# One core: softmax attention beside a spectral filter; how the first weights are fetched, when a score tile lends its third bank, and the order at the end

## The chip, the cores and the metric

The kernel runs on one core of a Trainium2 chip. The metric is the time of one execution on the device in microseconds (us); the median of four runs of the kernel before is 454.83 us (454.6 to 455.17). TensorE (PE) multiplies matrices into PSUM, which has eight banks of 512 float32 columns; ScalarE (ACT) computes functions, here the exponentials; VectorE (DVE) and GpSimd (POOL) do elementwise work; SyncE (SP) and ScalarE each have a queue for DMAs. The engines run side by side and wait for one another by semaphores.

## What is computed

```python
def _A_ref(x, wqkv, wo):                      # x: 1 x 2048 x 448, 16 heads of 28
    qkv = (x @ wqkv).reshape(B, S, 3, H, Dh)...
    p = softmax(einsum("bhqd,bhkd->bhqk", q, k) * Dh ** -0.5)
    return (p @ v, heads joined) @ wo
def _B_ref(x, w_r, w_i):                      # x: 1 x 2048 x 448
    return irfft2(rfft2(x) * (w_r + 1j * w_i))
out = concatenate([a, b], axis=-1)            # bfloat16
```

## The kernel before

`build_kernel` is its own planner. While it builds the program it keeps an estimated clock for each engine (`P.free`) and writes one instruction stream per engine, waits included; the order on each engine is fixed by then. The costs in the code (`mm_cost`, `cost=`) only steer that order.

**Attention.** The heads are four groups of four. A *unit* is the score of one head for 128 keys and 512 queries, one bank; there are 1024 units. `emit_tile` (its matmuls are L989) issues a tile of two or three units into the banks of its parity: even tiles use banks 0 to 2, odd tiles 3 to 5. One ScalarE instruction (L1002) then exponentiates the whole tile into `ET`, 1024 or 1536 columns, so a tile's banks are refilled while ScalarE works on the other parity's. Some units are not given to ScalarE: `choose` picks them and `start_d`/`finish_d` compute the exponential for pairs of them on DVE and POOL into `DE` (L1028, L1056, L1059, L1063, L1067, L1072, L1077). `emit_pv` (L1113) multiplies four units with V into bank 6; after 16 such groups the sums are normalized (`finish`).

**Jobs.** Everything else that TensorE does is a list of jobs with due times: transposes of x (L380), projections of q, k and v (L434, L452, L469, L486), the transforms of the spectral part (L655, L720, L774, L801, L837) and output projections (`o_job`, L1217). A job needs a bank for its sum: bank 7, or one that a score tile lends. `lend(t)` decides whether tile t gives up its third bank, and is then a two-bank tile; before tile `NT0` = 30 it always does. The lent bank is `lent[0]`. A job that is `SLIP` = 9 slots behind its due time counts as a reason to lend.

**Activity.** The planner adds up what TensorE streamed in the last 3.41 us. Below `TGT` x 4096 it starts jobs ahead of their due times; below `DUM` x 4096, with room left, it issues a filler, a matmul on zeros (`dummy`, L506).

**Head.** SP loads the first quarter of x (L344) and then the q and k columns of `wqkv`, rows 0 to 383, in one DMA (L349); ScalarE's queue loads the identity `cid` (L339) and rows 384 to 447 (L351). Then come the other quarters of x, the v columns, B's x and the constants. TensorE issues fillers, transposes the first quarter of x (L518), issues four fillers, and projects in three steps (`first_mm`, L434): keys 0 to 127 of head group 0, its queries 0 to 511, its other keys. POOL spreads k columns of `wst` into the padded `wk` (`spread`, recorded at L335): first those of group 0, then, after two of the four fills of `Vaug`, those of groups 1 to 3; then it fills `wo` and issues its four loads. Copies go through the helper `copy`, so they carry lines L333 (ACT) and L335 (DVE, POOL).

**Tail.** After the last score tile the main loop goes on until all PV groups and jobs are out. `ahead_o` may issue the first three of the four matmuls of an output tile (L1124) while it waits. `final_finish` handles the last 512 queries: first it finishes a job that is under way, then come the copies of the sums (`oaug`), the sums of the softmax by matmul (L1158), the reciprocals (L1163), their spread (`rzrep`, L1170), the normalized values (`onrm`, L1172), the last output matmuls (L1124), four evacuations and four DMAs.

Of the kernel before, what the change touches and what calls it, by code (L numbers as in the profile page):

```python
# [8 lines left out]
ALU = mybir.AluOpType  # L9
# [187 lines left out]
def build_kernel(nc, A_x, A_wqkv, A_wo, B_x, B_w_r, B_w_i, out):  # L197
    NG = 4
    UN = 1024
# [12 lines left out]
    DT0 = 30  # L212
    EARLY = 1
    TAILU = 8
    TGT = 1.05
    DUM = 0.95
    DROOM = 1.0
    PROOM = 6.0

# [14 lines left out]
    ROOMX = 0.0  # L234
    ZGAP = 9.0
    ALT = 0
    ODUE = 2
    POOLMID = -9.0

# [9 lines left out]

    ZRUN = 5  # L250

    SLIP = 9
    scale = float(DH) ** -0.5
    y16 = scale * 1.4426950408889634 * 65536.0
    bf16np = mybir.dt.np(BF16)
# [13 lines left out]
    ctx = ExitStack()  # L269
    with ctx:  # L270
        sem_names = ["pe", "act", "dve", "pool"]
        sem_names += ["d_x%d" % i for i in range(4)] + ["d_w", "d_wv", "d_wo", "d_c0", "d_c1", "d_t1", "d_t2", "d_xb"]
        sem_names += ["d_f%d" % i for i in range(4)] + ["d_wb%d" % i for i in range(2)] + ["d_o%d" % i for i in range(4)]
        P = Prog(nc, {n: ctx.enter_context(nc.semaphore("s_" + n)) for n in sem_names})

# [66 lines left out]
        def load_x(n):  # L342

            P.dma("sp", lambda e: e.dma_start(xa[:, 4 * n:4 * n + 4, :], A_x[0][512 * n:512 * n + 512, :].rearrange("(p c) d -> p c d", p=128)),  # L344
                  "d_x%d" % n, reads=[("xa", 0)] * (n == 1), writes=[("xa", n)], kb=448)

        load_x(0)
        load_c(0, 1, "cid", "act")
        P.dma("sp", lambda e: e.dma_start(wst[:, 0:3, :], A_wqkv[0:384, 0:896].rearrange("(c p) k -> p c k", p=128)),  # L349
              "d_w", writes=[("w", 0)], kb=672)  # L350
        P.dma("act", lambda e: e.dma_start(wst[64:128, 3, :], A_wqkv[384:448, 0:896]), "d_w", writes=[("w", 1)], kb=112)  # L351
        load_x(1)
        P.dma("sp", lambda e: e.dma_start(wv[:, 0:3, :], A_wqkv[0:384, 896:1344].rearrange("(c p) k -> p c k", p=128)),
              "d_wv", writes=[("wv", 0)], kb=336)
        P.dma("sp", lambda e: e.dma_start(wv[64:128, 3, :], A_wqkv[384:448, 896:1344]), "d_wv", writes=[("wv", 1)], kb=56)
        load_x(2)
        load_x(3)
        load_c(1, 3, "cid2")

        P.op("dve", lambda e: e.memset(zero[:], 0.0), writes=["zero"], cost=0.3)  # L360
# [2 lines left out]
        def spread(eng, g0, g1, part):  # L363

            off = 448 + 112 * g0
            nh = 4 * (g1 - g0)
            if part == 0:
                d_ = wk[:, 0:3, g0:g1, :].rearrange("p c g (j k) -> p c (g j) k", j=4)[:, :, :, 0:DH]
                s_ = wst[:, 0:3, off:off + DH * nh].rearrange("p c (j k) -> p c j k", j=nh)
            else:  # L370
                d_ = wk[64:128, 3, g0:g1, :].rearrange("p g (j k) -> p (g j) k", j=4)[:, :, 0:DH]
                s_ = wst[64:128, 3, off:off + DH * nh].rearrange("p (j k) -> p j k", j=nh)
            copy(eng, d_, s_, [("w", part), "wk", "wk0"], [("wk0" if g0 == 0 else "wk", part)], 0.12 * nh / 4 * (3 - 2 * part) + 0.1)

        def xt_mms(n, hf):
            mms = []
# [65 lines left out]
        def proj_qk(g, n, is_q, due, eng="dve"):  # L442
            mms = []
            if is_q:
                wkeys = [("w", 0), ("w", 1)]
                for c in range(4):
                    mms.append(lambda e, M, c=c: q_mm(e, M, g, c, 512 * n, 512 * (n + 1)))
            else:
                wkeys = [("wk0" if g == 0 else "wk", c) for c in range(2)]
                for c in range(4):  # L450
                    rlo, rhi, _ = crow[c]
                    mms.append(lambda e, M, c=c, rlo=rlo, rhi=rhi: e.matmul(  # L452
                        M, wk[rlo:rhi, c, g, :], xAT[rlo:rhi, c, 512 * n:512 * (n + 1)], start=(c == 0), stop=(c == 3)))
# [70 lines left out]
        def first_mm(col, m, i, lo, hi):  # L524
            for c in range(4):
                P.op("pe", lambda e, c=c: head_mm(e, bank(i), col, m, c, lo, hi),
                     reads=[("xAT0", c), ("w", c // 3)], writes=[("B", i)], cost=max(mm_cost(hi - lo), 0.18), act=hi - lo)


        first_mm(448, DH, 4, 0, 128)  # L530
# [97 lines left out]
        for h in range(2):  # L628
            for i in range(4):
# [7 lines left out]
                dve_task(lambda e, h=h, cs=cs, lo=lo, hi=hi: e.tensor_tensor(xf[h][:, cs, 225:448], lo, hi, ALU.subtract), rd, key[1], 0.5)  # L637
                dve_task(lambda e, h=h, cs=cs, src=src: e.tensor_copy(xf[h][:, cs, 0:225:224], src[:, cs, 0:225:224]), rd, key[2], 0.1)


        nB = [0]
# [284 lines left out]
        def lend(t):  # L926

            if t < NT0:
                return True
            other = bank_of(t + 1, 2)  # L930
            if lent[0] == other and vacant(other) and vacant(7):
                return False
            return sum(1 for jb in jobs if jb.due + SLIP <= pslot() and startable(jb) and order_ok(jb)) > (cur[0] is None)
# [205 lines left out]
            return True  # L1139

        def final_finish():

            while cur[0] is not None:
                step_job()

            def fill(keys):
                while len(obank) < 4 and P.free["pe"] + 0.5 <= P.ready("pe", keys):
# [199 lines left out]
        while pos() < UN or pvptr[0] < UN or jobs or cur[0] is not None:  # L1347
# [47 lines left out]
                    continue  # L1395
            if pos() >= UN and not jobs and cur[0] is None and len(obank) < 4 and pv_at > now + 0.5 and ahead_o():
                continue
            if tasks and now > max(TASK0, P.free[tasks[0][0]] + 0.3) and (tasks[0][0] == "pool" or P.free["pool"] <= now + CLASH):
                tasks.pop(0)[1]()
            low = P.activity(now) < TGT * 4096  # L1400
# [68 lines left out]
```

## Time and profile before

| | |
|---|---|
| median of 4 runs | 454.83 us |
| the profiled execution | 454.77 us |
| its span, first to last instruction | 453.0 us |
| granted TensorE clock, 10 to 445 us | 1.00 in every stretch asked |
| first exp starts | 9.77 us |
| last exp starts and ends | 444.31, 445.33 us |
| ACT busy, 9.77 to 45.28 us | 32.92 us (35 instructions) |
| ACT busy, 45.28 to 445.33 us | 399.00 of 400.05 us (361 instructions) |
| longest sum of waits of PE | L989 for ACT L1002: 28.7 us in 82 waits |
| DMA, first two slices of 11 us | 293 and 395 GB/s |

The span is the time from the first to the last instruction of the profiled execution; the execution's own time is 1.8 us longer. Busy time is a union, so two overlapping instructions count once. A row of the groups by shape reads: line, engine, operation, output <- input, shapes, count | busy time, mean duration in ns | idle time of the engine just before them and what ended it. A row of the timeline reads: start, duration, engine, line, operation, tiles, count, and in brackets the idle time before it with what ended it; neighbouring instructions of a line are merged, and then the duration is that of the whole row and the shape that of the first.

### The profile page before, as it was taken

How to read it: one execution, taken by the hardware profiler on the slowest of the kernel's cores; microseconds unless marked ns; L12 is line 12 of the kernel's file. 1: busy time of each engine (PE TensorE's matmuls, PEld its weight loads, DVE VectorE, ACT ScalarE, POOL GpSimd, SP SyncE). 2: the span in 40 equal slices, each digit the busy share in tenths (PEclk: the TensorE clock that was granted, in tenths of full speed). 3: DMA queues.
4: the chain of work that ended last, by engine and by line, in shares of the span. 5: the costliest groups of instructions: out<-in, count | busy, mean ns of one | idle time of the engine just before them, and what ended most of it. 6: DMA issues, size and time to landing. Idle time of an engine off the chain costs nothing.

```text
span 453.0 us, 8441 instructions
## 1 busy us (share of the span) xinstructions
PE 407.8 (90%) x3316; PEld 139.8 (31%) x3349; DVE 325.9 (72%) x575; ACT 437.4 (97%) x403; POOL 132.7 (29%) x122
## 2 busy tenths in 40 slices
PE   8999888888899898988899988887899889999997
PEld 3442322323233322323233223332243223232322
DVE  3346867776987887655587876666689888878783
ACT  4989999999999999999999999999999999999995
POOL 4800102003120215457622245654312111013210
PEclk9999999999999999999999999999999999999999
DMA  8921000000400120002100200000000130221012
GB/s 293 395 47 27 6 1 1 0 1 1 134 1 2 36 88 10 1 3 93 42 2 0 94 1 1 1 1 0 1 2 2 38 97 26 83 79 42 32 42 81
DMA packets 13415, 20.51 MB, mean 45 GB/s; under 512 B 5584, under 2 KB 10832, under 8 KB 12864
## 3 DMA queue, kind: packets, MB, share of 16 engines
q1 hardware_dynamic: 12816, 19.31, 12.9%
q8 instruction: 26, 0.43, 0.4%
q0 software_dynamic: 192, 0.40, 0.4%
q10 hardware_dynamic: 368, 0.26, 0.2%
q14 instruction: 13, 0.11, 0.1%
HBM read 16.30 MB, written 3.67 MB: 44 GB/s over the span
## 4 chain that ended last, share of the span: by engine, by line
ACT 46%; PE 42%; issue 10%; DVE 1%; ACTq 0%; DVEq 0%
ACT ET L1002 46%; PE PS L989 14%; PE PS L1113 6%; PE PS L655 4%; PE PS L837 3%; PE PS L801 3%; PE PS L434 2%; PE PS L506 2%; PE PS L469 2%; PE PS L452 1%; PE PS L486 1%; PE PS L1217 1%; PE PS L380 1%; PE PS L1124 1%; PE PS L774 1%
## 5 line engine op out<-in xcount | busy, mean ns | idle before, releaser
L1002 ACT ACTIVATE ET<-PS 128x1024 bf16<-128x1024 f32 (+1 forms) x394 | 431.9, 1287 | 4.2 <-PE PS L989 3.7
L989 PE MATMUL PS<-qT,kT 32*128 32x512 bf16 x1024 | 154.4, 385 | 31.9 <-ACT ET L1002 28.7
L1056 POOL TENSOR_SCALAR XT<-XI 128x1024 f16<-128x1024 uint16 (+1 forms) x40 | 50.9, 1271 | 221.3 <-DVE XI L1028 122.3
L1113 PE MATMUL PS<-ET,Vaug 128*32 128x512 bf16 x946 | 83.6, 386 | 5.0 <-ACT ET L1002 3.7
L989 PEld LDWEIGHTS PS<-qT,kT 32*128 32x128 bf16 x1024 | 37.9, 91 | 150.0 <-ACT ET L1002 129.7
L1028 DVE TENSOR_SCALAR XI<-PS 128x512 int32<-128x512 f32 x78 | 53.5, 685 | 21.4 <-PE PS L989 20.9
L1077 DVE SCALAR_TENSOR_TENSOR DE<-XI,XW 128x1024 uint16<-128x1024 int32 (+1 forms) x40 | 49.6, 1241 | 0.4
L749 POOL TENSOR_TENSOR ptmp<-R,WT 113x512 f32<-113x512 bf16 (+1 forms) x24 | 27.5, 1153 | 42.4 <-DVE DE L1077 41.6
L655 PE MATMUL PS<-FR,R 128*112 128x512 bf16 (+2 forms) x128 | 38.4, 397 | 0.5 <-issue 0.3
L837 PE MATMUL PS<-R,FR 128*128 128x448 bf16 x128 | 32.0, 356 | 0.1
L1113 PEld LDWEIGHTS PS<-ET,Vaug 128*32 128x32 bf16 x946 | 18.4, 94 | 38.2 <-issue 24.3
L1067 DVE TENSOR_TENSOR XT<-XT,XG 128x1024 f16<-128x1024 f16 (+1 forms) x40 | 27.0, 674 | 0.6
L1072 DVE TENSOR_TENSOR XW<-XT,XW 128x1024 f16<-128x1024 f16 (+1 forms) x40 | 26.8, 669 | 0.3
L1059 DVE TENSOR_SCALAR XG<-XT 128x1024 f16<-128x1024 f16 (+1 forms) x40 | 18.1, 454 | 9.4 <-POOL XT L1056 9.4
L1113 PE MATMUL PS<-DE,Vaug 128*32 128x512 bf16 x78 | 24.1, 385 | 0.4 <-ACT ET L1002 0.4
L335 DVE CAST Vaug<-PS 128x336 bf16<-128x336 f32 (+1 forms) x20 | 10.6, 529 | 18.8 <-PE PS L486 9.5
L434 PE MATMUL PS<-xAT,wst 128*32 128x512 bf16 (+5 forms) x288 | 22.1, 373 | 0.1
L335 DVE CAST qT<-PS 128x512 bf16<-128x512 f32 (+1 forms) x16 | 11.1, 691 | 14.3 <-PE PS L434 12.6
L506 PE MATMUL PS<-zero 128*128 128x512 bf16 x55 | 19.8, 412 | 0.7 <-issue 0.6
L659 DVE CAST R<-PS 112x512 bf16<-112x512 f32 (+2 forms) x16 | 11.0, 690 | 11.6 <-PE PS L655 11.3
L1195 POOL TENSOR_SCALAR rzrep<-rz 128x512 bf16<-128x512 bf16 x15 | 11.6, 774 | 24.9 <-DVE rz L1193 24.9
L655 PEld LDWEIGHTS PS<-FR,R 128*112 128x112 bf16 (+2 forms) x128 | 13.7, 130 | 16.2 <-issue 11.3
(86 smaller groups left out, 381.4 us busy)
## 6 DMA issues: line engine op xcount, KB each, us to landing
FR<-cst_f SPq DMA_DIRECT2D x4, 1024.0 KB, 8.1
FR<-cst_f SPq DMA_DIRECT2D x8, 512.0 KB, 3.5
out_dram<-astg SPq DMA_DIRECT2D x31, 112.0 KB, 1.7
R<-in_A_x_dram SPq DMA_DIRECT2D x4, 448.0 KB, 4.5
R<-in_B_x_dram SPq DMA_DIRECT2D x2, 896.0 KB, 8.3
wst<-in_A_wqkv_dram SPq DMA_DIRECT2D x1, 672.0 KB, 5.6
Wst<-in_B_w_r_dram SPq DMA_DIRECT2D x2, 225.0 KB, 8.7
Wst<-in_B_w_i_dram SPq DMA_DIRECT2D x2, 225.0 KB, 2.8
```

The lines of the kernel that those rows point to most:

```text
L434: ins = e.matmul(M[32 * j:32 * j + m, 0:hi - lo], wflat[rlo:rhi, o:o + m], xAT[rlo:rhi, c, lo:hi], start=(c == 0), stop=(c == 3), tile_pos ...
L506: P.op("pe", lambda e: e.matmul(bank(i), zero[:, :], zero[:, 0:1].to_broadcast([128, 512]), start=(i != 6), stop=(i != 6)), reads=["zero"] ...
L655: mms.append(lambda e, M, c=c: e.matmul(M[0:dn[b], :], xf[h][:, c, dlo[b]:dlo[b] + dn[b]], F1v[:, i, c, :], start=(c == 0), stop=(c == 7)))
L749: ptasks.append(("pool", reads, lambda: P.op("pool", lambda e: e.tensor_tensor(out_, in0, in1, ALU.mult), reads=reads + ["port"], writes=w ...
L837: mms.append(lambda e, M, r=r, tt=tt, n=n: e.matmul(M[:, 0:448], F2v[:, a % 4, r, tt, :], Y[:, tt, r, :], start=(n == 0), stop=(n == 7)))
L989: ins = e.matmul(bank(banks[i]), kT[32 * j:32 * j + 32, g % 2, 128 * kc:128 * (kc + 1)], qT[32 * j:32 * j + 32, (4 * g + qc) % 3, :], star ...
L1002: P.op("act", lambda e: e.activation(ET[:, s0:s0 + n, :], PS[:, b0:b0 + 512 * n].rearrange("p (a k) -> p a k", a=n), ACT.Exp, scale=scale) ...
L1028: P.op("dve", lambda e: e.tensor_scalar(xi, bank(bk), y16, 127.0 * 65536, ALU.mult, ALU.add), reads=[("B", bk)], writes=[("XI", x)], cost= ...
L1056: gps(lambda e: e.tensor_scalar(out_, lo, a / 65536, b, ALU.mult, ALU.add), [("XI", x)], key, 0.06 + 0.52 * f)
L1067: vec(lambda e: e.tensor_tensor(xt, xt, xg, ALU.mult), kt + kg, kt, 0.14 + 0.31 * f)
L1077: vec(lambda e: e.scalar_tensor_tensor(de[:, c], XI[x][:, c], 1.0 / 512, xw[:, c], ALU.mult, ALU.add), [("XI", x)] + kw, kd[lo:hi], 0.17 + ...
L1113: ins = e.matmul(ACC[32 * j:32 * j + 32, :], Vaug[:, g, kc, 32 * j:32 * j + 32], DE[:, dslot[u], :] if u in dslot else ET[:, place[u], :], ...
```

## The change

The q and k columns now come in eight DMAs instead of two: the first 116 columns of q on SP's queue and of k on ScalarE's queue, where the old loads stood, and the other 332 of each on SP's queue, behind the last quarter of x. Each part has its own semaphore, and readers wait for the part and half that they read. `lend` refuses an even tile while a bank is out (`LPOL` = 3). The main loop starts no job that would run past the moment at which the last PV group can start, and `final_finish` no longer finishes a job first. `TGT`, `DUM` and `SLIP` are lower. Three tasks that prepare the spectral part also wait for the readers of the buffer that they overwrite.

```diff
-    TGT = 1.05
-    DUM = 0.95
+    TGT = 1.02
+    DUM = 0.93
...
+    LPOL = 3
...
-    SLIP = 9
+    SLIP = 6
...
+        def load_qk(eng, t, lo, hi):
+
+            at = slice(448 * t + lo, 448 * t + hi)
+            n = "w%d" % (lo > 0)
+            P.dma(eng, lambda e: e.dma_start(wst[:, 0:3, at], A_wqkv[0:384, at].rearrange("(c p) k -> p c k", p=128)),
+                  "d_" + n, writes=[(n, 0, t)], kb=0.75 * (hi - lo))
+            P.dma(eng, lambda e: e.dma_start(wst[64:128, 3, at], A_wqkv[384:448, at]), "d_" + n, writes=[(n, 1, t)], kb=0.125 * (hi - lo))
+
         load_x(0)
         load_c(0, 1, "cid", "act")
-        P.dma("sp", lambda e: e.dma_start(wst[:, 0:3, :], A_wqkv[0:384, 0:896].rearrange("(c p) k -> p c k", p=128)),
-              "d_w", writes=[("w", 0)], kb=672)
-        P.dma("act", lambda e: e.dma_start(wst[64:128, 3, :], A_wqkv[384:448, 0:896]), "d_w", writes=[("w", 1)], kb=112)
+        load_qk("sp", 0, 0, 116)
+        load_qk("act", 1, 0, 116)
         load_x(1)
...
         load_x(2)
         load_x(3)
+        for t in range(2):
+            load_qk("sp", t, 116, 448)
         load_c(1, 3, "cid2")
...
-            copy(eng, d_, s_, [("w", part), "wk", "wk0"], [("wk0" if g0 == 0 else "wk", part)], 0.12 * nh / 4 * (3 - 2 * part) + 0.1)
+            copy(eng, d_, s_, [("w0", part, 1), "wk", "wk0"] + [("w1", part, 1)] * (g0 > 0), [("wk0" if g0 == 0 else "wk", part)], 0.12 * nh / 4 * (3 - 2 * part) + 0.1)
...
-                wkeys = [("w", 0), ("w", 1)]
+                wkeys = [(w, c, 0) for w in ("w0", "w1")[:1 + (g > 0)] for c in range(2)]
...
-                     reads=[("xAT0", c), ("w", c // 3)], writes=[("B", i)], cost=max(mm_cost(hi - lo), 0.18), act=hi - lo)
+                     reads=[("xAT0", c), ("w0", c // 3, col // 448)], writes=[("B", i)], cost=max(mm_cost(hi - lo), 0.18), act=hi - lo)
...
             other = bank_of(t + 1, 2)
+            if LPOL == 2 and t % 2 == 0:
+                return False
+            if LPOL == 3 and t % 2 == 0 and lent[0] is not None:
+                return False
             if lent[0] == other and vacant(other) and vacant(7):
                 return False
...
         def final_finish():
-
-            while cur[0] is not None:
-                step_job()
...
             if pos() >= UN and not jobs and cur[0] is None and len(obank) < 4 and pv_at > now + 0.5 and ahead_o():
                 continue
+            if pos() >= UN and pvptr[0] == UN - 4 and pv_at > now:
+                room = pv_at
```

In the three prepared tasks `rd` becomes `rd + over` in the second and third (`over` was in the first alone).

The built program differs from the one before in these counts: exps of two banks 209 (236), of three banks 177 (158); units computed on DVE and POOL 75 (78); fillers on zeros 69 (81); evacuations of output tiles 14 on DVE and 2 on ACT (13 and 3). TensorE's order is the same up to the spreading of the first softmax sums, at about 45 us.

More of the change, by code (lines that the diff above doesn't have):

```diff
@@ L271, in build_kernel @@
         sem_names = ["pe", "act", "dve", "pool"]
-        sem_names += ["d_x%d" % i for i in range(4)] + ["d_w", "d_wv", "d_wo", "d_c0", "d_c1", "d_t1", "d_t2", "d_xb"]
+        sem_names += ["d_x%d" % i for i in range(4)] + ["d_w0", "d_w1", "d_wv", "d_wo", "d_c0", "d_c1", "d_t1", "d_t2", "d_xb"]
         sem_names += ["d_f%d" % i for i in range(4)] + ["d_wb%d" % i for i in range(2)] + ["d_o%d" % i for i in range(4)]
@@ L636, in build_kernel @@
                 dve_task(lambda e, h=h, cs=cs, lo=lo, hi=hi: e.tensor_tensor(xf[h][:, cs, 1:224], lo, hi, ALU.add), rd + over, key[0], 0.5)
-                dve_task(lambda e, h=h, cs=cs, lo=lo, hi=hi: e.tensor_tensor(xf[h][:, cs, 225:448], lo, hi, ALU.subtract), rd, key[1], 0.5)
-                dve_task(lambda e, h=h, cs=cs, src=src: e.tensor_copy(xf[h][:, cs, 0:225:224], src[:, cs, 0:225:224]), rd, key[2], 0.1)
+                dve_task(lambda e, h=h, cs=cs, lo=lo, hi=hi: e.tensor_tensor(xf[h][:, cs, 225:448], lo, hi, ALU.subtract), rd + over, key[1], 0.5)
+                dve_task(lambda e, h=h, cs=cs, src=src: e.tensor_copy(xf[h][:, cs, 0:225:224], src[:, cs, 0:225:224]), rd + over, key[2], 0.1)
         nB = [0]
```

## The prediction

> **What bounds the kernel now.** I read the busy shares first, then ScalarE's instructions by shape, then what ended ScalarE's idle time, then the timeline at both ends.
>
> ```profile
> PE 407.8 (90%) x3316; PEld 139.8 (31%) x3349; DVE 325.9 (72%) x575; ACT 437.4 (97%) x403; POOL 132.7 (29%) x122
> ...
> ACT 46%; PE 42%; issue 10%; DVE 1%; ACTq 0%; DVEq 0%
> ```
>
> ScalarE is busy 97% of the span. The chain of waits gives it only 46% because it changes to TensorE at each small wait; the two hand the score banks to each other.
>
> ```profile
> L1002 ACT ACTIVATE ET<-PS 128x1024 bf16<-128x1024 f32 x236 | 233.9, 1099 | 4.0 <-PE PS L989 3.5
> L1002 ACT ACTIVATE ET<-PS 128x1536 bf16<-128x1536 f32 x158 | 225.8, 1568 | 0.2 <-PE PS L989 0.2
> ```
>
> 236x2 + 158x3 = 946 score units are exponentiated here; the other 78 of 1024 go to VectorE. Records overlap, so a tile's cost is read from start to start: three-bank tiles average 1.334 us, two-bank tiles 0.952. The shortest are 1.330 and 0.903; what lies above is time in which TensorE had not yet refilled the banks, nearly all of it behind two-bank tiles (236 of them idle 4.0 us, 158 three-bank ones 0.2, the rest hidden in overlapping records).
>
> ```profile
> 43.02 11.77 ACT L1002 ACTIVATE ET<-PS 128x1024 bf16<-128x1024 f32 x9
> ```
>
> The 33rd two-bank tile starts at 43.02, and eight three-bank ones follow it. The last exp ends at 444.31 + 1.02 = 445.33. So 445.33 - 43.02 - 1.02 = 401.29 us are 203 two-bank and 158 three-bank steps; at 1.334 the latter are 210.8, which leaves 0.938 for a two-bank step in this stage. The 32 steps before it take (43.02 - 9.77)/32 = 1.039: there TensorE is full of projections.
>
> Head and tail are the two stretches without exps, 9.77 us and 453.0 - 445.33 = 7.7 us:
>
> ```profile
> 4.52 1.48 PE L518 MATMUL PS<-cid,R 128*128 128x128 bf16 x16
> 5.17 1.25 ACT L333 ACTIVATE xAT<-PS 128x512 bf16<-128x512 bf16 x2 [2.06 <-PE PS L518]
> 5.84 1.03 PE L506 MATMUL PS<-zero 128*128 128x512 bf16 x4
> 6.85 0.46 POOL L335 COPY wk<-wst 128x336 bf16<-128x336 bf16 x1 [6.40 <-DMA wst<-in_A_wqkv_dram]
> 6.93 2.47 PE L434 MATMUL PS<-xAT,wst 128*28 128x128 bf16 x48
> 9.77 4.74 ACT L1002 ACTIVATE ET<-PS 128x1024 bf16<-128x1024 f32 x5 [0.59 <-PE PS L989]
> ...
> 43.50 1.03 POOL L1056 TENSOR_SCALAR XT<-XI 128x1024 f16<-128x1024 uint16 x1 [22.40 <-DVE XI L1028]
> ```
>
> The weights are there at 6.85 (POOL's wait), the first projection starts at 6.93. But the four fillers ahead of it begin at 5.84 and hold TensorE nearly as long.
>
> ```profile
> 444.90 0.93 PE L1217 MATMUL PS<-wo,onrm 128*128 128x448 bf16 x4
> 445.76 0.40 PE L1113 MATMUL PS<-ET,Vaug 128*32 128x512 bf16 x4
> 446.22 0.42 DVE L335 CAST oaug<-PS 128x256 bf16<-128x256 f32 x1 [1.57 <-PE PS L1113]
> 448.43 1.49 PE L1124 MATMUL PS<-wo,onrm 128*128 128x448 bf16 x7
> 448.70 0.42 DVE L1172 TENSOR_TENSOR onrm<-oaug,PS 128x256 bf16<-128x256 bf16 x1 [0.42 <-PE PS L1170]
> 449.83 0.54 ACT L333 ACTIVATE astg<-PS 128x448 bf16<-128x448 f32 x1 [0.40 <-PE PS L1124]
> 450.02 0.62 DVE L335 CAST astg<-PS 128x448 bf16<-128x448 f32 x1 [0.32 <-PE PS L1124]
> ```
>
> Four L1217 matmuls stand ahead of the last PV, which starts 0.43 us after the last exp's end; then seven L1124 matmuls lead to the last two evacuations.
>
> **Head.** Before, 784 KB of q and k columns came in two DMAs; now the first 116 columns of each come first, 87 + 14.5 KB per queue, 203 KB in all. Gain: TensorE could go on when its fillers are through. A further 512-column matmul in a row costs 0.22 us (two L452 take 0.61, one 0.39), so the four fillers are through at 5.84 + 4x0.22 = 6.72. So at most 6.93 - 6.72 = 0.21 us, and the rest of the earlier landing lies beside fillers and the xAT copies (ScalarE's second ends at 5.17 + 1.25 = 6.42). When do the weights land? The identity load, 256-byte runs on ScalarE's queue beside x, landed 3.7 us after its issue. The second weight DMA of each queue should issue near 1.7 (the first issues began at 1.16 and 1.19 and took 0.64 and 0.43), so 5.4; 203 KB behind x at the first slice's 293 GB/s add 0.7: 6.1. The other bound is the old load's 5.6 us from an issue at 2.3: 7.9, a loss of 1.0. I take -0.2, since the new runs resemble the identity's. The Trainium skill speaks against this edit: "DMA: Bandwidth & Descriptors", Specifications, asks for 512 bytes or more per run for line rate and says shorter ones are read, modified and written. These are 232 bytes; at half rate, my estimate from that page, the load would take 1.4 instead of 0.7 and still land at 6.8, leaving 0.1 of the gain.
>
> Costs: four further SP issues of some 0.43 to 0.55 us stand before cid2 and the B_x load, which move back 1.9 us: B_x landed about 15.7 (issue 7.34, 8.3 to land), its first reader L624 runs at 30.79. POOL's second spread now waits for the late columns, until 12.4 to 17 by the landings of neighbours (5.6 and 8.3 after 6.9 to 8.8); behind it stand two Vaug fills, the wo fill and four wo DMAs, 22.4 - 11.35 = 11 us before POOL is idle, so idle at 28 at worst. POOL's next work is at 43.50 and Vaug groups 1 to 3 are first written at 40.52, so nothing. Without that cover, each microsecond beyond 40 would hold V projections.
>
> **Middle.** TensorE's order is unchanged up to the tile at about 45 us, so the slow 33 tiles stay. After that the built program has 209 two-bank and 177 three-bank exps instead of 236 and 158, because even tiles lend less; VectorE takes 75 units instead of 78. ScalarE: -27x0.938 + 19x1.334 = -25.33 + 25.35 = 0.0. At the shortest steps, that is if the waits stay in total, -27x0.903 + 19x1.330 = +0.9. If I sort the excess of each step by the shapes of the tiles around it and carry it to the new sequence, the waits fall from 7.3 to 6.3: -0.1. I take -0.1. Other bounds: half of the 7.3 us gone is -3.6 + 0.9 = -2.7; a third more of them is +0.9 + 2.4 = +3.3. VectorE and POOL lose three units' work and TensorE 12 fillers (12x0.22 = 2.6 us); these engines are not the bound, so that is only slack.
>
> TGT and DUM lower the wished activity of TensorE by 3% and 2%. Before, the granted clock is 1.00 in every stage from 10 to 445 us, although stretches of 3.4 us in the trace carry only 0.63 to 0.79 of the planner's 4096 instead of the wished 0.95; laid against the tile order, the new program's thin stretches are alike. So cost zero; the price of one half-clock stretch is in the rivals. Here the skill also warns: "TensorE: Matmul & The Clock Gate", Part 1, has a free-running window of about 3.4 us after which a quiet TensorE falls to half clock. By it one such window is possible; the trace shows none.
>
> **Tail.** In the new order TensorE has, after its last score tile, one PV group, six L1124 matmuls (two output banks), then three PV groups, the first of them all from VectorE. Let the third-last exp start at a: the last starts at a + 0.91 + 1.33 and ends at a + 3.26. The last scores issue when the third-last exp ends, a + 1.1; PV 0.22, six L1124 at 0.19 (seven take 1.49, one 0.35) = 1.14: TensorE is at a + 2.7. VectorE's last DE: the last o_job's evacuation can begin near a + 0.15 and takes 0.62, DE 1.23: a + 2.1, so 0.6 of cover; a DE later than that is paid one for one. Two PV groups to a + 3.1, and the last waits for the exp alone: other matmuls start 0.06 after an exp's end. With 0.1 instead of 0.43: -0.33. Next, the last L1124 row has four matmuls instead of seven, the three of the fourth bank having been done earlier. Before, the third output's last matmul was sixth, 448.43 + 5x0.19 = 449.38; now only the second onrm holds it, 448.70 + 0.42 + 0.06 = 449.18: -0.2. Both evacuations and the DMA follow. The L1217 evacuation goes from ScalarE (445.95, off the path) to VectorE. Tail -0.5; bounds 0 (DE late) and -0.6.
>
> Sum: -0.2 - 0.1 - 0.5 = -0.8. The profiled execution took 454.77 (span 453.0, 1.8 around it), 0.06 below the median of 454.83. So 454.0.
>
> **Rivals.**
> 1. The waits melt: with three-bank tiles in the even places too, TensorE has 0.4 us more before each bank is due, and most stalls of 0.1 to 0.3 us go. For: the three-bank steps show nearly none. Against: many two-bank pairs remain. 1.2 us more gain: 452.8.
> 2. Slower: jobs short of a bank. Even tiles lend only while none is out, so a projection or transform job waits for bank 7 to be evacuated (0.69 us of VectorE) and is then pressed between scores; the stalls behind such rows are 0.2 to 0.33 us (after four L801 and eight L1113 one is 0.33). For: fewer lent banks, fewer offloaded units. Against: TensorE is 90% busy and the tail holds no more left-over jobs than before. Three more such stalls eat the gain, from seven on it is slower than before; ten at 0.26: 456.6 - with two or three fewer two-bank stalls, 455.9.
> 3. The clock falls once in 3.4 us: TensorE, 92% full there, needs 1.84 times as long, 0.84x3.4 = 2.9 us: 456.9. Decided by one slice below full clock.
> 4. The edits at head and tail do nothing: weights behind their many small runs, DE late: -0.1 in all, 454.7.
>
> **How the numbers follow.** A change under 0.2% (0.9 us) can hardly be told from none. Chances: forecast 0.42 (453.2 to 454.8), melting waits 0.22, bank shortage 0.18, clock 0.05, nothing 0.13. Faster than 453.92: half of the forecast and rival 1, 0.44; slower than 455.74: rivals 2 and 3, 0.21; the rest, 0.35. The range 452.4 to 456.2 leaves out the far ends.
>
> **What would show it.** Right: L434 at 6.7, first exp near 9.55; L1002 with 209 and 177, idle before it no longer than 4.2; last PV within 0.15 us of the last exp's end; the last row of output matmuls four long, tail 7.2 us. Wrong: POOL's first copy after 6.9, an exp stretch other than 435.5 by over 0.7 us, a clock below 1.00, a PV that waits for DE.

## The result, and the profile after

The changed kernel takes 454.2 us (median of 38 runs, 453.08 to 454.55), the kernel before, run beside it, 455.09 (median of 56, 454.5 to 458.1). The recorded ratio is 0.9971, 95% interval [0.9963, 0.9979]; it weighs all runs, the long ones of the kernel before too, and the medians alone give 0.9980. The forecast was 454.0. The profiled executions hit the sum less well: the head gained more than forecast, the exp stretch lost instead of gaining, and the two errors partly cancel.

| us | before | after | forecast of the step | seen |
|---|---|---|---|---|
| first exp starts | 9.77 | 9.10 | -0.2 | -0.67 |
| first exp's start to last exp's end | 435.56 | 436.33 | -0.1 | +0.77 |
| last exp's end to the span's end | 7.62 | 7.07 | -0.5 | -0.55 |
| profiled execution | 454.77 | 454.31 | -0.8 | -0.46 |

The page of the changed kernel: busy shares, the granted clock in 40 slices, the chain of waits.

```profile
PE 405.7 (90%) x3310; PEld 137.8 (30%) x3337; DVE 317.9 (70%) x563; ACT 437.4 (97%) x394; POOL 130.4 (29%) x120
...
PEclk9999999999999999999999999999899999999999
...
PE 44%; ACT 43%; issue 8%; DVE 4%; DVEq 0%; ACTq 0%
```

ScalarE is as busy as before. New is one 8 in the row of clocks. The exps by shape:

```profile
L1016 ACT ACTIVATE ET<-PS 128x1536 bf16<-128x1536 f32 x177 | 252.7, 1592 | 0.6 <-PE PS L1003 0.5
L1016 ACT ACTIVATE ET<-PS 128x1024 bf16<-128x1024 f32 x209 | 210.3, 1107 | 3.7 <-PE PS L1003 3.3
```

The counts are the planned 177 and 209, and two-bank tiles idle 3.7 instead of 4.0 us. Next the stretches of 3.41 us around the 8 (columns: stretch and its length, then for PE, PEld, DVE, ACT and POOL busy us and instructions, then granted clock, DMA share, GB/s):

```profile
318.44:321.86 3.42, 3.22 (x40) 1.01 (x39) 2.65 (x5) 3.42 (x4) 1.05 (x1) 1.00 0.02 5
321.86:325.27 3.41, 2.09 (x24) 0.63 (x22) 2.95 (x4) 3.41 (x4) 0.00 (x0) 1.00 0.00 0
325.27:328.69 3.42, 3.42 (x20) 0.63 (x17) 1.54 (x3) 2.92 (x3) 1.77 (x2) 0.50 0.00 0
328.69:332.10 3.41, 3.41 (x31) 2.11 (x28) 1.84 (x6) 3.19 (x4) 0.54 (x1) 1.00 0.00 0
```

In the second row TensorE is busy 2.09 of 3.41 us; in the third it has half its clock for exactly that length, and ScalarE, full in the two rows before, idles 0.49 us there and 0.22 in the next. The head and the tail (timeline: start, duration, engine, line, operation, tiles, shape, count, idle before):

```profile
4.38 1.08 PE L528 MATMUL PS<-cid,R 128*128 128x128 bf16 x16
4.83 1.09 ACT L334 ACTIVATE xAT<-PS 128x512 bf16<-128x512 bf16 x2 [1.26 <-PE PS L528]
5.25 0.46 POOL L336 COPY wk<-wst 128x336 bf16<-128x336 bf16 x1 [4.80 <-DMA wst<-in_A_wqkv_dram]
5.30 1.03 PE L516 MATMUL PS<-zero 128*128 128x512 bf16 x4
6.26 2.48 PE L444 MATMUL PS<-xAT,wst 128*28 128x128 bf16 x48
9.10 1.02 ACT L1016 ACTIVATE ET<-PS 128x1024 bf16<-128x1024 f32 x1 [0.59 <-PE PS L1003]
...
443.28 1.22 DVE L1091 SCALAR_TENSOR_TENSOR DE<-XI,XW 128x1024 uint16<-128x1024 int32 x1
443.79 1.31 PE L1138 MATMUL PS<-wo,onrm 128*128 128x448 bf16 x6
445.03 0.40 PE L1127 MATMUL PS<-DE,Vaug 128*32 128x512 bf16 x4
445.48 0.10 PEld L1127 LDWEIGHTS PS<-ET,Vaug 128*32 128x32 bf16 x4 [0.33 <-ACT ET L1016]
445.94 0.42 DVE L336 CAST oaug<-PS 128x256 bf16<-128x256 f32 x1 [1.44 <-PE PS L1127]
448.90 0.55 PE L1138 MATMUL PS<-wo,onrm 128*128 128x448 bf16 x2 [0.21 <-DVE onrm L1183]
449.36 0.54 ACT L334 ACTIVATE astg<-PS 128x448 bf16<-128x448 f32 x1 [0.21 <-PE PS L1138]
```

The weights are there at 5.25 (POOL's wait), not 6.1. The transposes begin 0.14 us earlier than before and take 1.08 instead of 1.48 us, so the fillers begin at 5.30 instead of 5.84 and the first projection at 6.26. In the tail the last PV's weights load at 445.48, 0.05 after the last exp's end (445.43), and the last output matmuls come as two (from 448.15) and two (from 448.90). VectorE's last DE is done at 443.28 + 1.22 = 444.50, 0.53 before TensorE comes to it at 445.03.

A whole profile at full clock is what separates the terms; runs below give it. In what follows the *exp stretch* is the time from the first exp's start to the last exp's end, the *tail* what is left from there to the span's end, and the *release* the moment in the head at which the granted clock rises from half to full.

### The profile page after: what moved, and what is told of

Its sections match the earlier page's. It is cut to its first block, busy times and chain, and to the rows that moved or that the text cites. A ratio compares the mean times of both kernels' runs of the same rounds, so it can differ in the third digit from the quotient of the medians.

```text
span 452.5 us, 8388 instructions
## 1 busy us (share of the span) xinstructions
PE 405.7 (90%) x3310; PEld 137.8 (30%) x3337; DVE 317.9 (70%) x563; ACT 437.4 (97%) x394; POOL 130.4 (29%) x120
## 4 chain that ended last, share of the span: by engine, by line
PE 44%; ACT 43%; issue 8%; DVE 4%; DVEq 0%; ACTq 0%
ACT ET L1016 43%; PE PS L1003 14%; PE PS L1127 6%; PE PS L665 5%; PE PS L847 4%; PE PS L811 2%; PE PS L444 2%; PE PS L479 2%; PE PS L516 2%; PE PS L462 1%; PE PS L496 1%; PE PS L784 1%; PE PS L1228 1%; PE PS L390 1%; PE PS L1138 1%
## 5 line engine op out<-in xcount | busy, mean ns | idle before, releaser
L1003 PE MATMUL PS<-qT,kT 32*128 32x512 bf16 x1024 | 152.2, 386 | 32.1 <-ACT ET L1016 29.1
L1070 POOL TENSOR_SCALAR XT<-XI 128x1024 f16<-128x1024 uint16 (+1 forms) x38 | 49.3, 1298 | 191.8 <-DVE XI L1042 118.2
L1042 DVE TENSOR_SCALAR XI<-PS 128x512 int32<-128x512 f32 x75 | 51.4, 685 | 22.6 <-PE PS L1003 21.3
L1091 DVE SCALAR_TENSOR_TENSOR DE<-XI,XW 128x1024 uint16<-128x1024 int32 (+1 forms) x38 | 46.2, 1216 | 0.6
L1081 DVE TENSOR_TENSOR XT<-XT,XG 128x1024 f16<-128x1024 f16 (+1 forms) x38 | 25.8, 678 | 0.6
L1086 DVE TENSOR_TENSOR XW<-XT,XW 128x1024 f16<-128x1024 f16 (+1 forms) x38 | 25.6, 674 | 0.4
L336 DVE CAST kT<-PS 128x512 bf16<-128x512 f32 (+2 forms) x17 | 11.2, 660 | 18.2 <-PE PS L462 17.3
L1127 PE MATMUL PS<-DE,Vaug 128*32 128x512 bf16 x75 | 22.9, 386 | 0.0
L336 DVE COPY Esb<-PS 128x225 f32<-128x225 f32 (+2 forms) x24 | 11.8, 490 | 12.2 <-PE PS L811 5.8
L1073 DVE TENSOR_SCALAR XG<-XT 128x1024 f16<-128x1024 f16 (+1 forms) x38 | 15.8, 415 | 4.4 <-POOL XT L1070 4.4
```

The lines of the kernel that those rows point to most:

```text
L336: P.op(eng, lambda e: e.tensor_copy(dst, src), reads=reads, writes=writes, cost=cost)
L1003: ins = e.matmul(bank(banks[i]), kT[32 * j:32 * j + 32, g % 2, 128 * kc:128 * (kc + 1)], qT[32 * j:32 * j + 32, (4 * g + qc) % 3, :], star ...
L1042: P.op("dve", lambda e: e.tensor_scalar(xi, bank(bk), y16, 127.0 * 65536, ALU.mult, ALU.add), reads=[("B", bk)], writes=[("XI", x)], cost= ...
L1070: gps(lambda e: e.tensor_scalar(out_, lo, a / 65536, b, ALU.mult, ALU.add), [("XI", x)], key, 0.06 + 0.52 * f)
L1081: vec(lambda e: e.tensor_tensor(xt, xt, xg, ALU.mult), kt + kg, kt, 0.14 + 0.31 * f)
L1091: vec(lambda e: e.scalar_tensor_tensor(de[:, c], XI[x][:, c], 1.0 / 512, xw[:, c], ALU.mult, ALU.add), [("XI", x)] + kw, kd[lo:hi], 0.17 + ...
```

## The experiments

All were run beside the kernel before, 12 runs each (6 of f2 and of m1); a ratio is to that. A mean granted clock of 0.994 to 0.996 is one half-clock stretch of 3.41 us and some of the last microseconds; 0.997 or more has none before the tail.

**h1_before_new_loads** and **h2_after_old_loads**: loads crossed with order. The kernel before with the eight new weight DMAs, and the changed kernel with the two old ones; every other instruction in the order of its own kernel.

```diff
 h1, in before.py; planned with the old loads' times, issued:
         load_x(0); load_c(0, 1, "cid", "act")
+        cut("sp", 0, 0, 116, "w0"); cut("act", 1, 0, 116, "w0")
...
+        for t in range(2): cut("sp", t, 116, 448, "w1")
 h2, in after.py; planned with the new loads' times, issued:
+        old_loads()
```

> The order of every compute instruction is that of the kernel before; only the weight DMAs are those of the change. Theory A (the loads are worth what the fillers leave free): first exp 0.2 us earlier than 9.77, time 0.2 us under before (ratio 0.9995). Rival B (the loads bring the whole shift seen in the changed kernel, whose first exp started at 9.10): first exp near 9.1, time 0.7 us under before (0.9985). Rival C (a shift in the head is eaten later): first exp earlier, time as before.

> The order of every compute instruction is that of the changed kernel; only the weight DMAs are the old two. Theory A: 0.2 us more than the changed kernel (454.2 by its median), so ratio to before about 0.9975. Rival B: 0.7 us more, ratio about 0.9987. If middle and tail bring nothing (the loads are all of the gain), ratio 1.000.

h1 took 454.96 us, ratio 0.9985 [0.9963, 1.0007]; h2 454.12, ratio 0.9974 [0.9955, 0.9994]. By its median h2 is as fast as the changed kernel, and h1's median is that of the kernel before it stood beside (454.97), though its fastest run is at 454.0 and theirs at 454.56. So most of the gain seems to be in the order of the middle and the tail, and the loads help in some runs only; the times alone don't prove it, since h1's interval holds both a ratio of 1 and the changed kernel's. The profiles say more. Both have full clock from the head to 450 us: h1's exp stretch is 435.64 and its tail 7.64, like those of before; h2's are 435.28 and 7.07.

Why in some only is read from the start of the first projection, which the first exp follows by 2.83 or 2.84 us in every profile with the four fillers (6.26 and 9.10 in the changed kernel). In h1, released at 5.90, it is 6.97, later than the 6.93 of before, though POOL had its weights at 5.24: the four fillers end only there. In h2 it is 7.51: the clock was released only at 7.02, and the fillers themselves ran at half speed (1.50 us for four, 1.03 at full).

```profile
5.98 0.26 PEld L533 LDWEIGHTS PS<-zero 128*128 128x128 bf16 x2
6.09 1.50 PE L533 MATMUL PS<-zero 128*128 128x512 bf16 x4
7.30 0.46 POOL L336 COPY wk<-wst 128x336 bf16<-128x336 bf16 x1 [6.85 <-DMA wst<-in_A_wqkv_dram]
7.51 2.47 PE L461 MATMUL PS<-xAT,wst 128*28 128x128 bf16 x48
10.35 1.02 ACT L1033 ACTIVATE ET<-PS 128x1024 bf16<-128x1024 f32 x1 [0.59 <-PE PS L1020]
```

**c1_fill_gaps**: the changed kernel with 18 more matmuls on zeros in nine thin places, put where TensorE waits anyway.

```diff
+        PV_FILL = {57: 2, 181: 2}
+        TILE_FILL = {123: 2, 436: 3, 485: 2, 570: 1, 576: 1, 621: 3, 739: 2}
...
+                P.streams["pe"].append(lambda e: e.matmul(bank(6), zero[:, :], zero[:, 0:1].to_broadcast([128, 512]), start=False, stop=False))
...
+            more(TILE_FILL.get(scores[0], 0))
...
+            more(PV_FILL.get(u0 // 4 + 1, 0))
```

> The changed kernel with 18 further fillers on zeros, put only where TensorE waited 0.2 to 0.95 us for ScalarE inside its nine thinnest stretches. Theory A (the one stretch at half clock in the profiled run, 325.3 to 328.7, costs 0.7 to 0.9 us, and comes from a thin window): granted clock 1.00 before the end in all runs and 453.5 us by median, ratio 0.9955 or lower, no run at 454.3. Rival (half clock there costs nothing because ScalarE is the bound, or it has another cause): the clock still falls in some runs or the time stays at 454.2.

453.81 us, ratio 0.9969 [0.9954, 0.9983]; 11 of 12 runs without a half-clock stretch in the middle (of the changed kernel 26 of 38). The theory had none at 454.3 or above; one run, at 454.55 and clock 0.994, is. Over all runs of this order, 22 of 74 without the 18 fillers (the changed kernel, h2, w1, w2) have a half-clock stretch in the middle and 2 of 24 with them (c1, f1). Its profile: first exp 9.75, exp stretch 435.20, tail 7.09. Laid exp by exp against h2, which has the same order, and counted from the first exp, c1 differs by no more than 0.2 us but for one exp near 278 us (0.36). The changed kernel runs within 0.02 us of c1 up to 320 us and is 1.1 us later from 340 on. That is the price of the one half-clock stretch: 436.33 - 435.20 = 1.13. The middle at full clock is therefore 0.36 us shorter than before.

**t1_no_ahead**: the changed kernel without the six output matmuls ahead of the last PVs.

```diff
-            if pos() >= UN and not jobs and cur[0] is None and len(obank) < 4 and pv_at > now + 0.5 and ahead_o():
+            if pos() >= UN and not jobs and cur[0] is None and len(obank) < 4 and pv_at > now + 0.5 and False:
```

> The changed kernel, but no output matmuls are issued before the last PV groups: the order of the last row of output matmuls is again 3, 3, 3, 7 instead of 6 ahead of PV, then 3, 3, 4. Theory A (the tail's second term is the three matmuls in front of the third output): the last PV within 0.15 us of the last exp's end as in the changed kernel, from there to the span's end 0.2 us longer; time 0.2 us above the changed kernel. Rival (the DMA's landing or the evacuations on DVE set the end): no difference over 0.05 us.

454.44 us, ratio 0.9968 [0.9949, 0.9988]: the times can't tell it from the changed kernel. Its tail is 7.25 instead of 7.07. The lines that decide:

```profile
444.48 0.10 PEld L1127 LDWEIGHTS PS<-DE,Vaug 128*32 128x32 bf16 x4 [0.67 <-DVE DE L1091]
445.42 0.40 PE L1127 MATMUL PS<-ET,Vaug 128*32 128x512 bf16 x4 [0.32 <-ACT ET L1016]
448.08 1.49 PE L1138 MATMUL PS<-wo,onrm 128*128 128x448 bf16 x7
449.48 0.54 ACT L334 ACTIVATE astg<-PS 128x448 bf16<-128x448 f32 x1 [0.40 <-PE PS L1138]
```

The last row is seven long again, and costs 0.18 us (7.25 - 7.07). The last PV starts 0.06 after the last exp's end (445.36) here too. What is left, 7.62 - 7.25 = 0.37, is that the last PV has nothing of a job in front of it. The first line shows VectorE's cover from the other side: without the six matmuls TensorE waits 0.67 us for DE, until 444.48.

As for the edit that is to do this: the changed kernel built without its lines on the tail (the job limit in the main loop and the loop in `final_finish`) has the same instructions in the same order on every engine. The new order at the end comes from the plan of the middle, which leaves no job over; the edit itself moves nothing in this kernel. m1 below, which has the old lines, ends alike: its last PV starts 0.05 us after the last exp's end, its last row is seven long, and its tail is 7.25, not the 7.6 that was expected of it.

**f1_no_head_fillers**: c1 without the four zero matmuls of the head; the planner still counts them, so that the rest keeps its order.

```diff
-        dummy(7, 4)
+        for _ in range(4):
+            planned_only(7)
```

> c1_fill_gaps with the four zero matmuls between the last xAT transpose and the first projection taken out; everything behind them is in the same order. In the changed kernel they begin at 5.30 and hold TensorE until the first projection at 6.26, though the weights are spread from 5.25 to 5.71 and the xAT copies end at 4.83 + 1.09 = 5.92 (ScalarE). Theory (TensorE's fillers are now the limit of the head, as the prediction said of 6.72): the first projection starts about 0.3 us earlier against the same phase of the clock's release, first exp 0.2 to 0.35 us earlier (about 8.8 to 9.4 by the phase), and the time is 0.2 to 0.35 us under c1, so 453.5. Rival 1: the four fillers carry the activity by which full clock is released; without them the release comes later or lapses, the head's projections run at half clock and the first exp is 0.5 to 1.5 us later: 454.3 to 455.3. Rival 2: the copies of xAT are the limit, not the fillers: no change, 453.8.

**f3_before_no_head_fillers**: the same edit in the kernel before.

> The kernel before without the four zero matmuls ahead of its first projection; the order of all else is the same. Theory (in the kernel before the weights' landing at 6.85 holds the first projection nearly as long as the fillers do, so the fillers' time can be had only with the split loads): first projection no earlier than 6.85, time -0.1 to 0 against before, 454.7 to 454.9. Rival 1 (the fillers cost by themselves, through the clock's release or what is queued behind them, whenever the weights land): -0.5 as f1_no_head_fillers has against c1_fill_gaps, 454.3. Rival 2 (fewer fillers put the release off): first exp later, 455.3 or more.

f1 took 453.26 us, ratio 0.9959 [0.9944, 0.9974], 11 of 12 runs between 452.64 and 453.47; f3 454.80, ratio 1.0003 [0.998, 1.0025]. So no cost of the fillers is seen with the old loads, where the interval leaves about 1 us either way, and with the new ones they cost 0.55 us (453.81 - 453.26), more than the 0.2 to 0.35 expected. f3's head and then f1's:

```profile
4.29 1.06 PE L525 MATMUL PS<-cid,R 128*128 128x128 bf16 x16
6.90 0.46 POOL L335 COPY wk<-wst 128x336 bf16<-128x336 bf16 x1 [6.46 <-DMA wst<-in_A_wqkv_dram]
6.99 2.48 PE L434 MATMUL PS<-xAT,wst 128*28 128x128 bf16 x48 [1.64 <-DMA wst<-in_A_wqkv_dram]
9.82 1.02 ACT L1010 ACTIVATE ET<-PS 128x1024 bf16<-128x1024 f32 x1 [0.59 <-PE PS L997]
```

```profile
4.38 1.91 PE L535 MATMUL PS<-cid,R 128*128 128x128 bf16 x16
5.26 0.46 POOL L336 COPY wk<-wst 128x336 bf16<-128x336 bf16 x1 [4.81 <-DMA wst<-in_A_wqkv_dram]
6.22 2.83 PE L444 MATMUL PS<-xAT,wst 128*28 128x128 bf16 x48
9.41 1.02 ACT L1034 ACTIVATE ET<-PS 128x1024 bf16<-128x1024 f32 x1 [0.59 <-PE PS L1019]
```

f3's clock was released at 4.18, its transposes took 1.06, and still TensorE waits 1.64 us for the weights. f1 is the other extreme, a release at 6.96 and transposes of 1.91, and it starts its first projection at 6.22 where h2, at a release of 7.02, has 7.51. That execution is the one of f1's 12 with half-clock stretches in the middle (455.8 us; two, from 290.26 to 297.09). No thin stretch stands in front of them: in the 3.41 us before the fall TensorE is busy 3.01 us, 88%. And h2 keeps its full clock behind a stretch that is only 62% busy, 2.12 of 3.41 us. Both stretches are counted from the release in steps of 3.413 us. The rows of f1, then those of h2:

```profile
286.85:290.26 3.41, 3.01 (x27) 1.15 (x27) 2.03 (x4) 3.41 (x4) 2.78 (x3) 1.00 0.00 0
290.26:293.67 3.41, 3.41 (x23) 1.26 (x22) 2.49 (x7) 3.00 (x3) 1.05 (x1) 0.50 0.00 0
```

```profile
324.46:327.87 3.41, 2.12 (x16) 0.70 (x17) 2.91 (x4) 3.41 (x4) 0.94 (x1) 1.00 0.00 0
327.87:331.29 3.42, 3.42 (x34) 1.79 (x32) 1.62 (x4) 3.42 (x4) 1.37 (x2) 1.00 0.00 0
```

So the busy share of the stretch before doesn't settle alone whether the clock falls.

**f2_no_mid_fillers**: the changed kernel with its 57 zero matmuls of the middle planned and not issued.

```diff
-                    dummy(spare[0] if spare else 6)
+                    planned_only(spare[0] if spare else 6)
```

> The changed kernel with none of its 57 zero matmuls of the middle issued; the order of all else is the same. Theory (the half-clock stretch of 3.4 us at 325 follows a quiet TensorE, and the fillers are what keeps TensorE busy enough; TGT and DUM set their number): half clock in every run, in several stretches of 3.4 us, mean granted clock 0.97 or lower; each stretch costs 0.7 to 0.9 us as the one of the changed kernel does, so with 5 to 10 stretches 457 to 462. By the price of the prediction's rival (2.9 us each) it would be 468 or more. Rival (the drops come of themselves, whatever TensorE does): one drop or none as in the changed kernel, and the time is the same, 453.7 to 454.5, or up to 0.3 us less since TensorE has 57 matmuls fewer.

482.06 us by the median of all six runs (474.26 to 494.37); the recorded ratio, 1.0458 [1.0408, 1.0508], is that of the two shortest, 474.26 and 478.31. The order of all else is the same. The row of clocks of its profile, an execution of 474.26:

```profile
PEclk9999779999999989999995879995656999999999
```

24 stretches of 3.41 us are at half clock there, alone or in runs of up to eight, and against h2 exp by exp they cost 21.0 us, 0.88 each. So 57 matmuls that compute nothing are worth 20 us in the shortest run and 28 by the medians. The price per stretch was expected well; the number, and so the time, was far beyond the 5 to 10 stretches given.

**m1_no_middle_edits**, **m2_lending_back**, **s1_slack_back**: the changed kernel, planned anew, with all the edits but the loads undone, with the rule for lending undone, and with `SLIP` undone.

```diff
 m1:
-    TGT = 1.02
-    DUM = 0.93
-    LPOL = 3
-    SLIP = 6
+    TGT = 1.05
+    DUM = 0.95
+    SLIP = 9
 (and the tail's edit and the added waits undone)
 m2:
-    LPOL = 3
+    LPOL = 0
 s1:
-    SLIP = 6
+    SLIP = 9
```

> The changed kernel with TGT, DUM, SLIP, the rule for lending and the tail's edit as before; only the split weights are left, planned anew: 202 two-bank and 183 three-bank exps, 72 units on VectorE, a last row of seven output matmuls as before. Theory (the middle's time is the sum over exps by the prediction's step prices): -34 x 0.938 + 25 x 1.334 = +1.46 us against the kernel before in the exp stretch, so 437.0; head -0.2, tail as before 7.6; time 454.8 - 0.2 + 1.45 = 456.05. Rival (the middle's time is set by waits that follow the edits to lending and slack, not by the count of exps): a stretch like before's, 435.6, and 454.6.

> The changed kernel with the rule for lending as before, planned anew: 243 two-bank and 154 three-bank exps, 77 units on VectorE, tail in the new order. Theory (step prices): +7 x 0.938 - 4 x 1.334 = +1.23 us against the kernel before, stretch 436.8, tail 7.1, head -0.2: 454.8 - 0.2 + 1.2 - 0.55 = 455.25. Rival (the rule for lending does nothing for the time by itself): the stretch of the changed kernel at full clock, 435.2, and 453.7. Second rival (the two-bank waits grow with their number, +0.14 us more by the neighbours of each exp): 455.4.

> The changed kernel with SLIP 9 as before, planned anew: 200 two-bank and 183 three-bank exps, 75 units on VectorE, the tail with six output matmuls in it ahead of the last PVs (three and three) and a last row of four. Theory (step prices, if the clock stays full): -36 x 0.938 + 25 x 1.334 = -0.42 us against the kernel before, stretch 435.1, tail 7.1, head -0.2: 453.7. Second theory (what m1_no_middle_edits showed: the clock decides; each half-clock stretch of 3.41 us costs 1.1 to 1.5): the plan has thin places as m1 has, and each window lost adds 1.1 to 1.5 to 453.7; one window 455, three 458. The page's PEclk row tells which. Rival (less slack only reorders): as the changed kernel with one drop in a third of the runs, 453.6 to 454.5.

| | median, us | ratio | exp stretch expected, full clock | exp stretch in the profile | half-clock stretches in the middle |
|---|---|---|---|---|---|
| m1 | 459.66 | 1.0088 [1.0068, 1.0108] | 437.0 | 440.72 | 3 in the profile; clock 0.988 or 0.989 in all 6 runs |
| m2 | 454.13 | 0.9972 [0.9957, 0.9988] | 436.8 | 436.10 | none in 12 runs |
| s1 | 454.82 | 0.9994 [0.9975, 1.0012] | 435.1 | 435.91 | one in 6 of 12 runs |

Counting exps by the prices of two- and three-bank steps gets the order m2 over s1 right and each to 0.8 us, no better. A part of m2's error is a count: its last exp is of one bank. Undoing the rule for lending costs 0.9 us of the exp stretch against c1 (436.10 - 435.20) and 0.3 us in medians; against the changed kernel itself, whose runs lose some clock, the medians show nothing (454.13 and 454.20). m1's theory and rival both fell, since neither foresaw the clock:

```profile
260.36:263.77 3.41, 2.03 (x19) 0.48 (x14) 2.67 (x5) 3.41 (x3) 1.45 (x1) 1.00 0.00 0
263.77:267.18 3.41, 3.06 (x22) 0.69 (x25) 1.83 (x4) 2.75 (x4) 0.70 (x1) 0.50 0.00 0
267.18:270.60 3.42, 3.42 (x25) 0.67 (x21) 0.87 (x2) 2.10 (x3) 0.23 (x1) 0.50 0.02 5
270.60:274.01 3.41, 3.41 (x22) 0.86 (x18) 2.01 (x3) 2.12 (x3) 0.00 (x0) 0.50 0.00 0
274.01:277.42 3.41, 2.51 (x27) 0.87 (x21) 1.42 (x3) 3.41 (x3) 3.10 (x3) 1.00 0.00 0
```

A TensorE busy 2.03 of 3.41 us is followed by three half-clock stretches, in which ScalarE loses 0.66, 1.32 and 1.29 us, 3.27 of the 3.7 between expected and measured. m1 wishes for more activity than the changed kernel does (1.05 and 0.95) and gets less at this place; the planner counts what it believes was streamed, but that this is the reason wasn't tested. s1's six runs with a stretch took 455.32 to 456.46, the six others 453.78 to 454.32: there one costs some 2.4 us between the medians. Undoing `TGT` and `DUM` alone, or the added waits alone, wasn't tried.

**w1_first_load_256** and **w2_first_load_all**: the changed kernel's order with a first load of 256 or all 448 columns of q and k instead of 116, on the same two queues; `load_qk` only plans its times here, and `cut` issues.

```diff
 w1:
+        cut("sp", 0, 0, 256, ("w0",))
+        cut("act", 1, 0, 256, ("w0",))
...
+            cut("sp", t, 256, 448, ("w1",))
 w2:
+        cut("sp", 0, 0, 448, ("w0", "w1"))
+        cut("act", 1, 0, 448, ("w0", "w1"))
```

> The changed kernel's order on every engine with the first 256 columns of q and k in the first load instead of 116: 512-byte runs, 448 KB instead of 203. Theory (bytes decide when it lands): 245 KB more at the 293 GB/s of the first slice are 0.84 us, POOL's first copy starts at 5.25 + 0.84 = 6.1 instead of 5.25; the first projection still waits for fillers or just for the weights, 6.3, and the time is the changed kernel's, 453.6 to 454.5. Rival (short runs go at half rate, so 203 KB in 232-byte runs cost what 406 KB would): POOL's first copy at 5.25 + 0.15 = 5.4 or earlier.

> As w1, with all 448 columns of q and k in the first load, 896-byte runs, 784 KB, on two queues (before: the same bytes in 1792-byte runs, one queue for each row group). Theory (bytes decide): 581 KB more are 2.0 us, POOL's first copy at 7.2, the first projection at 7.3 instead of 6.26, first exp about 1.0 us later at equal phase of the clock's release; 454.3 to 454.7, near h2_after_old_loads. Rival (landing is set by the fixed time of a DMA, not by its bytes): POOL's first copy before 6.0 and no change in time.

w1 453.62 us, ratio 0.9963 [0.9948, 0.9979]; w2 454.64, ratio 0.9983 [0.9968, 0.9998]. POOL's first copy is at 5.25 with 203 KB, 5.89 with 448 (w1) and 6.70 with 784 (w2):

```profile
5.89 0.46 POOL L336 COPY wk<-wst 128x336 bf16<-128x336 bf16 x1 [5.44 <-DMA wst<-in_A_wqkv_dram]
```

The bytes decide, at a lower price than expected (0.64 us instead of 0.84 for the first step, 1.45 instead of 2.0 for both); the rival that short runs cost as much as twice their bytes would have had 5.4. w1 is as good as the changed kernel; in its profile, released at 5.70, the fillers and not the weights hold the first projection.

## Why the prediction was right, and where not

**Head.** The mechanism was right: weights early, then TensorE held by its fillers until four of them are through. The size was not one number. The -0.2 was worked out from one profile, in which the clock was released at 5.44 and the fillers (to 6.72) and the weights (6.85) ended nearly together. The release moves from run to run; in the profiles here it came between 3.82 and 7.02 us. Early, the old weights are what is late, and the first projection starts at 6.99 (f3) against 6.26 (after): -0.7. Late, the fillers are: h2 waits for fillers until 7.51 though its weights were spread from 7.30, and w1, released at 5.70, has its first exp at 9.77, just where the kernel before has it, though its weights came 1 us earlier. The -0.67 seen is the early case. The landing was also mis-sized: 5.25 is earlier even than the 5.4 that was to hold without the bytes; the two first loads of 87 KB took 3.3 and 3.5 us from issue to landing, not 3.7 and 0.7 more. That the further issues on SP's queue and POOL's second spread cost nothing was right: counted from the first exp, c1 is level with h2, which has neither, at 40 us and stays 0.06 us or more ahead of it from 45 on.

The Trainium skill's "DMA: Bandwidth & Descriptors", Specifications, had been weighed against this: below 512 bytes a run is not at line rate. In the traces' DMA records a packet takes (median) 18 ns at 232 bytes and at 256, 27 at 512, 41 at 896, 74 at 1792, 140 at 3584. The rate per byte at 232 is indeed half of that at 3584 (12.9 against 25.6 bytes per ns). But nothing happens at 512: a fixed 8 ns and 0.037 ns per byte fit all six within 2 ns. 896 packets of 18 ns over 16 engines are 1.0 us, an estimate between the 0.7 I took and the 1.4 by the page. The first loads of w1 and w2 are the same 896 packets at 512 and 896 bytes; the estimate puts them 0.5 and 1.3 us later than the 232-byte ones, and 0.64 and 1.45 were measured.

**Middle.** At full clock -0.3 to -0.4 instead of -0.1 (h2 435.28 against before's 435.56; c1 435.20 against h1's 435.64). The same way of counting by steps missed m2 and s1 by 0.7 and 0.8 us, so that the -0.1 came this near is in part luck. Two-bank steps take 0.937 us in c1, 0.938 before: neither did the waits melt (rival 1), nor were jobs short of a bank (rival 2). Which of the edits brings the 0.36 us stays open: each of m1, m2 and s1 is another program.

**The clock** is the step that failed, in the words of the prediction: "So cost zero". It rested on one profile of before at 1.00 from 10 to 445 us. Of the runs of the kernel before that stood beside the experiments, 25 of 93 have a mean clock below 0.997, and the changed kernel has a half-clock stretch in 12 of 38. So rival 3 is not a case of 5 in 100 that befalls a whole kernel, but one that befalls some three runs in ten of either. Its price was wrong too: 1.1 us in the changed kernel's profile and 0.88 in f2, though some 2.4 in s1, where 2.9 were worked out, because I took TensorE as 92% full of work that ScalarE waits for. In the profile of the changed kernel part of what TensorE does in the lost stretch is fillers (three took 1.46 us of it) and what ScalarE doesn't wait for yet (0.49 and 0.22 us are lost in the two rows above, the rest behind them). The skill's warning, "TensorE: Matmul & The Clock Gate", Part 1, that the clock halves after one free-running window of some 3.4 us, is borne out in its length and its grid. Its word "idle" is not: the longest gap of TensorE in the 3.41 us before 325.27 is 0.62 us, and it was busy 61% of it. That too little work of TensorE lets the clock fall is shown by f2; which stretch is lost is not explained, as f1's fall behind 88% and h2's full clock behind 62% show.

**Tail.** -0.55 for -0.5. Both parts have the size worked out: the last PV 0.05 instead of 0.43 us after the last exp's end (-0.37 by t1), the last row of four instead of seven (-0.18 by t1; 0.2 was given), with the cover of DE 0.53 for 0.6. What was wrong is the edit that I credited with it: the tail follows from the plan of the middle, and m1 has the first part without it.

**Sum.** At full clock the profiled c1 stands 0.9 us below before, as -0.02, -0.36 and -0.53 add up; the changed kernel's 14 runs at clock 1.00 have a median of 453.62, below the forecast, and 12 with a half-clock stretch in the middle have 454.4. The other 12, at 0.997 or 0.998, have 454.35; that they are runs of a late release, as h2's profile at 0.998 is, is inferred. So the 454.0 was hit by a head and a middle taken too small and a clock taken too well.

**A better version.** f1, the changed kernel with 18 fillers more in the middle and four fewer in the head, has the lowest median here: 453.26 us. Its interval of the ratio, [0.9944, 0.9974], still overlaps that of the changed kernel, [0.9963, 0.9979]; but 11 of its 12 runs are below 453.5 and 4 of the changed kernel's 38.

## What to carry to other kernels

A step that depends on when the clock is released, or on whether one thin stretch loses it, has no single size: take several runs' clocks before writing "zero" beside it. Short waits can be enough: two profiles lost the clock behind 3.41 us in which TensorE was busy about 60% with no gap of 1 us, but no threshold came out of these runs. A filler is cheap where the engine waits anyway and dear where something is ready behind it: 57 of them are worth 20 us or more in the middle, four cost 0.55 in the head. Where a planner lays the whole program, undoing one edit makes another program; to test an edit, plan with it and issue without it.

## What the runs showed of the hardware that was not expected

- The changes of the clock lie on a grid that starts with its release. Releases at 4.42 (after), 4.36 (m1) and 6.96 (f1) are followed by the first fall at 325.27, 263.77 and 290.26: 94, 76 and 83 times 3.413 us later, and every other change in the 14 profiles lies on its run's grid too. That the same program falls or doesn't according to where the grid lies over its thin places would fit, but wasn't tested; why the grid lies where it does was not found.
- Between two executions of the same order at full clock, the starts of exps can agree to 0.002 us, counted from the first: c1 and w1 do at all 386, and c1's 18 fillers in gaps cost nothing. Both run 0.06 us ahead of h2 at nearly every exp from 77 to 417 us. In these profiles the larger differences come from the head's release and from lost stretches.
